# Bucket attention and eight experts on one core: weight pieces that follow ScalarE without a wait, a later closing, sums and opening in other places

## The chip, the core and the metric

The kernel runs on one core of one Trainium2 chip. The core has TensorE (PE, matrix products into PSUM), VectorE (DVE), ScalarE (ACT) and GpSimd (POOL), each with an instruction stream of its own, and SyncE (SP), which here only issues transfers. Semaphores order the streams. The metric is the device time of one execution in microseconds (us), median of the runs shown. "Clock" is the share of full speed that PE's throttle granted.

## The reference

An attention whose mask lets a query see only the keys with the same six sign bits, and behind it a mixture of eight experts of fixed capacity, with a greedy assignment over all scores:

```
q_bits = einsum(q, proj) > 0          # (4, 8, 768, 64) x (64, 6); k_bits alike
mask   = bucket(q_bits) == bucket(k_bits)
scores = where(mask, q @ k.T / 8, -1e9);  attn = softmax(scores);  x = attn @ v   # x: 3072 x 512

logits = x @ w_gate                   # 3072 x 8
for idx in argsort(-logits.flatten()):        # greedy, capacity 384 each
    tok, e = divmod(idx, 8)
    if assigned[tok] >= 0 or counts[e] >= cap: continue
    assigned[tok] = e; counts[e] += 1
for e in range(8):
    out[assigned == e] = relu(x[assigned == e] @ w1[e]) @ w2[e]     # 512 -> 1024 -> 512
```

All is float32. The kernel gets the precision from pairs of 16-bit numbers: a number is split into a high part (a cast, mostly on ACT) and a residue (`lo`, `vl`, `ql`, `kl`, `wl`: number minus high part), and a product is a sum of three 16-bit products.

## The kernel before

**Attention** handles 32 heads in 8 groups of four. A head is six steps (192 in all), each with two half-steps; a half-step is the unit in which the tables count. In a step PE computes one block of masked scores for the row maximum (L239, reduced by DVE in L241) and, some steps later, the transposed scores (`ST`, L257 and L258), whose exponentials ACT takes (L259); the residue `lo` is taken by POOL or DVE (L262), as the tables `PAT`, `E0`, `E1` say by head and step. Four steps later the products with the values follow (L272 to L274). `m_rows` (L243 to L248) writes a head's maxima through PE and ACT into the mask rows of `qa`, which `ST` reads. The three buffers called `pst` in PSUM are shared by `ST`, `m_rows`, the transposed outputs (`xtr`, L299 to L301), the sums and the first routing.

The loads, casts, subtractions and moves of the next group are put between the steps by tables: `P1`, `P2`, `P3` for groups 1 to 3, `P4` for the rest. `sumv` (L194 to L205) sums the values and their residues on PE, and `sumw` (L206 to L213) makes the weights of the mask rows from it: a product, ACT's copy `shi`, and one DVE step. Entry 18 of a table is the half-step of `sumv`, `SW` says how many later `sumw` comes, and `SU` places both for group 0. Before the first step stands the opening, whose order the string `OPS` writes out: `i` constants, `t` `b` casts and sign bits of head 0, `w` warm-up products of PE (no part of the result; `DW` counts a first lot and their width), `r` `l` casts and residues, `s` a score block, `B` `D` bits of head 1 and their transfers, `c` `u` `m` `d` `f` `v` `x` parts of group 0's preparation, `C` copies.

**The first routing** runs inside the last heads: `best` (L485) finds each token's best expert from the logits and makes the key that orders the tokens, in chunks as the batches are done; `compare` (L507) compares a digit of the key with thresholds.

**The experts** are eight blocks of 68 slots: 32 slots of layer 1, 36 of layer 2, three or two PE products in each. While block p-1 runs, the routing of phase p picks the 384 tokens of the next expert, in 14 steps (`phase`, L558) that the tables `EP` and `ES` put at slots: the first is the choice's first count, step 11 is the closing of the search (L636 to L662: the threshold, who is taken, which expert's weights come next), step 12 the places (L665), step 13 the collection (L677), behind which `end` issues the gather of the tokens and begins the next phase's choice. Phases of the table that are not in `EP` use `ES`.

A quarter of a weight matrix is cast by ACT (L757), scaled in place by a second pass of ACT (L766, at the end of `wsplit`), and then split by two pieces `wl`. Pieces wait in a list. `hand` (L771) gives the next n of them to POOL when a routing step has been issued; the counts per step are the tables `HP` (by phase) and `HS`. Ahead of them it puts a `tick` (L774), a copy of one element of the last routing result (`s.gate`), so that POOL does not start before DVE has that result. `fill` and `own` give pieces to DVE, and what is left goes to POOL at a due slot. POOL's queue also holds the scatters of the results (L839), the weight loads (L748) and the gathers (L740).

Of the kernel before, what the change touches and what calls it, by code (L numbers as in the profile page):

```python
# [20 lines left out]
 E0=[3, 5],  # L21
# [5 lines left out]
 DW=[5, 0, 0, 0, 384],  # L27
 P1=[13, 13, 14, 15, 17, 21, 23, 21, 16, 27, 21, 26, 23, 24, 33, 32, 3, 4, 46, -6, 3, 13],
 P2=[41, 44, 48, 49, 51, 51, 57, 55, 45, 49, 55, 57, 52, 60, 59, 60, 2, 3, 72, 32, 36, 47],
# [5 lines left out]
 SW=4,  # L35
# [4 lines left out]
 SU=13,  # L40
 OPS='b0 i3 i2 t0 b1 w5 r0 r2 w4 s0 w4 C1 r1 t1 c1 s1 B0 c0 D0 w2 w1 s4 w5 s2 s3 r3 v2 w5 v0 l0 l1 C0 m0 s5 w3 s6 r5 w2 l3 e0 e1 d0 u0 u1 s7 v1 l2 w0 m1 e2 | s8 | x0 | w0 | x1 s9 | r4 s10 | | | s11 m2 v3 f0 | x3 | | x2 | m3 | | | | | |')
# [4 lines left out]
def attention(tc, nc, ctx, qT, kT, vv, proj, wg, x_dram, L, jp, identf, B, late=None, after=None):  # L46
# [74 lines left out]

    TMP={}
# [8 lines left out]
    def bits(G,pairs):  # L131
# [12 lines left out]
        if G==0: V.tensor_scalar(bt[r],bt[r],8192.0,None,op0=ALU.mult)  # L144
# [172 lines left out]
    def copies(a):  # L317
# [4 lines left out]
        e=lambda k: ST(0,k,0),C=lambda n: copies((QA,KA)[n]),w=lambda n: warm(n,DW[4]))  # L322
# [6 lines left out]
    add(AP['WS'],wsplit); add(AP['SU'],sumv,0); add(AP['SU']+3,sumw,0)  # L329
# [38 lines left out]
    for t in range(6*NH+LAG+6):  # L368
        h,s=divmod(t,6)
        first=(t-LAG)%6==5  # L370
        if first: av(t)
        if t<6*NH and t not in early: ST(h,s,0)
        for x in S_at.get(t,[]): S_pass(*x)
        run(2*t)
        if h<NH: ST(h,s,1)
        if t>=1 and (t-1)//6<NH:
            hh,ss=divmod(t-1,6)
            lo(hh,ss,V if ss in (E0 if hh<1 else E1 if hh<2 else PAT[hh%2]) or t==6*NH else G_)
        run(2*t+1)
        if not first: av(t)  # L380
# [10 lines left out]
ES=[-16,-13,-11,-8,-2,1,5,8,12,15,19,22,28,36]  # L391
EP={1:E1,
# [3 lines left out]
WL=[4,46]  # L396
W1=[[],[57,66,70,74],[53,65,69,73],[50,57,62,67],[46,52,58,63],[44,52,58,63]]
HP={2:[0,0,0,3,1,2,2,2,2,0,0,0,0,0],3:[0,0,0,3,1,2,2,2,2,2,0,0,0,0],4:[0,0,0,3,0,3,0,3,1,2,0,0,0,0]}
HS=[0,0,0,3,0,3,0,2,2,2,0,0,0,0]
# [9 lines left out]
class Moe:  # L409
# [6 lines left out]
    def consts(s):  # L416
# [36 lines left out]
        s.identb=cp.tile([128,128],BF,name="identb")  # L453

        s.gp=cp.tile([128,2,2,NC],BF,name="gp")
        for i,v in enumerate((1.0,-1.0)):
            todo.append(lambda i=i,v=v: A.activation(s.gp[:,i,0,:],iof[:,0:NC],AF.Copy,scale=128.0*v))
            todo.append(lambda i=i,v=v: A.activation(s.gp[:,i,1,:],pcol.to_broadcast([128,NC]),AF.Copy,scale=v))
        s.th=iota([128,4,NC],[[128,4],[0,NC]],0,4097,name="th")
# [10 lines left out]
        todo.append(lambda: G_.tensor_scalar(s.identb,s.jp,0.0,None,op0=ALU.is_equal))  # L470
# [14 lines left out]
    def best(s,P,c0,c1,first=False):  # L485

        V=s.nc.vector; n=c1-c0; r=slice(c0,c1); L3=s.Lm[:,r]
        m,eq,mx,mxu,OH,key,D,E=(P[x] for x in ("m","eq","mx","mxu","OH","key","D","E"))
        def bc(ap): return ap[:,r,None].to_broadcast([128,n,8])
# [5 lines left out]
            lambda: V.tensor_tensor(eq[:,r],eq[:,r],wt,op=ALU.mult),  # L495
# [3 lines left out]
        if not first: todo.append(lambda: V.tensor_tensor(mxu[:,r],mx[:,r],s.un[:,r],op=ALU.mult))  # L499
        return todo+[  # L500
            lambda: V.tensor_tensor(E[:,0,r],D[:,0,r],s.sc[:,0,r],op=ALU.mult),
            lambda: V.tensor_tensor(OH[:,r],bc(mxu),wt,op=ALU.is_equal)]
# [4 lines left out]
    def compare(s,cmp,l,d,c0=0,c1=None,eng=None):  # L507
        J=NT[l]; tb=s.TB[l]
        o,i,b=s.paired(d,c0,s.NC if c1 is None else c1,J,cmp,tb)
        (eng or s.nc.vector).tensor_tensor(o,i,b,op=ALU.is_ge)  # L510

    def paired(s,d,c0,c1,J,out,tb):

        r=slice(c0//2,c1//2); sh=[128,c1//2-c0//2,J,2]
        return out[:,r],d[:,c0:c1].rearrange("p (s q) -> p s q",q=2)[:,:,None].to_broadcast(sh),tb[:,None].to_broadcast(sh)
# [20 lines left out]
    def early(s,b,ps,wps,nb=4):  # L536
# [9 lines left out]
        todo=s.best(s.Z,c0,c0+n,True)  # L546
        for a in range(c0,c0+n,6): todo.append(lambda a=a: s.compare(s.Z["cmp"][0],0,s.Z["E"][:,0],a,a+6))
# [310 lines left out]
    def run(s):  # L858
# [5 lines left out]
        def step(p,n):  # L864
            next(ch[p],None); s.hand(n)
# [82 lines left out]
```

## Time and profile before

| | us |
|---|---|
| median of 3 runs | 735.23 (734.71 to 735.5) |
| the profiled execution | 734.54 |
| its span | 732.8 |
| PE busy in the span | 673.7 (92%) |
| DVE, ACT, POOL busy | 519.3, 470.1, 525.4 |

The mean granted clock is 0.97. Attention with its opening takes until about 393 us, then comes a turn of some 30 us, and layer 1 of the eight blocks starts between 424 and 693 us. A timeline row has the start, the duration, the engine, the line, the operation with its output and inputs, and at the end, in brackets, how long the engine stood idle before it and what ended that. Rows that run without a hole are joined, with their number as x2 and the like.

### The profile page before, as it was taken

Reading aid. Unit: us, or ns where it says so; the run is one execution under the profiler, and the core shown is the slowest. Engines: PE = TensorE matmul, PEld = TensorE weight load, DVE = VectorE, ACT = ScalarE, POOL = GpSimd, SP = SyncE. Lnnn points to the kernel's source line nnn. Section 1 sums busy time; section 2 is a strip of 40 time slices with the busy share of each in tenths; the row PEclk is TensorE's granted clock in tenths of the full one; section 3 lists DMA queues with packets and bytes.
Section 4 is the critical chain, followed back from the end, with each engine's and each line's share of the span. In section 5 each row is a group of like instructions: output and inputs, shape, how many; then the busy total and the mean of one; then the engine's idle time right before and its main releaser. Section 6 shows DMA issues by size and latency. Waiting matters only on the chain. (4 is left out here: it accounts for less than half of the span.)

```text
span 732.8 us, 19247 instructions
## 1 busy us (share of the span) xinstructions
PE 673.7 (92%) x7865; PEld 433.4 (59%) x7865; DVE 519.3 (71%) x1124; ACT 470.1 (64%) x886; POOL 525.4 (72%) x486
## 2 busy tenths in 40 slices
PE   8899989999999999998997599989898989899995
PEld 2566656767767677676675464545454555545552
DVE  5868876878877878788965688697878787843120
ACT  7678776778978788776662172927373645556650
POOL 8589959998988979886772446575756473867761
PEclk9999999999999999999997599999999999999998
DMA  7638572726636255430000344435352526172601
GB/s 194 173 93 229 141 190 50 204 69 134 180 93 165 80 151 158 89 81 23 24 24 23 110 165 147 156 138 179 127 175 98 205 88 229 55 277 58 258 29 43
DMA packets 39952, 93.58 MB, mean 128 GB/s; under 512 B 4548, under 2 KB 30520, under 8 KB 37816
## 3 DMA queue, kind: packets, MB, share of 16 engines
q1 hardware_dynamic: 33048, 46.21, 24.2%
q0 software_dynamic: 6816, 46.15, 18.1%
q8 instruction: 61, 1.00, 0.6%
q14 instruction: 27, 0.22, 0.1%
HBM read 59.53 MB, written 12.58 MB: 98 GB/s over the span
## 5 line engine op out<-in xcount | busy, mean ns | idle before, releaser
L262 POOL TENSOR_TENSOR lo<-pt 128x768 f16<-128x768 f32 x143 | 229.7, 1621 | 40.6 <-ACT pt L259 33.0
L259 ACT ACTIVATE pt<-pst 128x384 f32<-128x384 f32 x384 | 181.1, 491 | 72.9 <-PE pst L258 63.3
L241 DVE TENSOR_REDUCE m<-pss 128x1 f16<-128x770 f32 x192 | 182.0, 957 | 51.8 <-PE pss L239 50.6
L257 PE MATMUL pst<-qa,ka 128*128 128x384 f16 x384 | 126.1, 329 | 7.3 <-ACT qa L248 4.0
L258 PE MATMUL pst<-qb,kb 128*128 128x384 f16 x384 | 125.8, 328 | 0.0
L274 PE MATMUL psv<-vh,lo 128*128 128x65 f16 x1152 | 121.7, 194 | 3.2 <-POOL lo L262 3.2
L273 PE MATMUL psv<-vl,pt 128*128 128x64 f16 x1152 | 121.9, 193 | 0.0
L272 PE MATMUL psv<-vh,pt 128*128 128x65 f16 x1152 | 121.9, 195 | 0.0
L272 PEld LDWEIGHTS <-pt 128*128 128x128 bf16 x1152 | 107.3, 98 | 11.2 <-issue 3.5
L273 PEld LDWEIGHTS <-pt 128*128 128x128 bf16 x1152 | 106.3, 99 | 8.0 <-issue 0.2
L274 PEld LDWEIGHTS <-lo 128*128 128x128 f16 x1152 | 106.3, 98 | 3.5 <-POOL lo L262 3.5
L239 PE MATMUL pss<-ka,qa 128*128 128x385 f16 x384 | 95.0, 330 | 0.4 <-DVE m L241 0.3
L757 ACT ACTIVATE wh<-wf 128x1024 f16<-128x1024 f32 x64 | 67.0, 1051 | 36.6 <-DMA wf<-in_w_dram,zwidx 34.3
L775 POOL TENSOR_TENSOR wl<-wf,wh 128x512 f16<-128x512 f32 x76 | 85.9, 1147 | 0.0
L818 PEld LDWEIGHTS <-wh 128*128 128x128 f16 x512 | 47.9, 98 | 33.4 <-issue 3.4
L830 PEld LDWEIGHTS <-hh 128*128 128x128 f16 x384 | 36.2, 98 | 40.7 <-issue 3.2
L833 ACT ACTIVATE o<-po 128x512 f32<-128x512 f32 x24 | 14.3, 595 | 70.7 <-PE po L830 60.4
L766 ACT ACTIVATE wf<-wf 128x1024 f32<-128x1024 f32 x55 | 58.0, 1055 | 1.0
L262 DVE TENSOR_TENSOR lo<-pt 128x768 f16<-128x768 f32 x49 | 56.8, 1159 | 1.5 <-ACT pt L259 1.0
L821 DVE SCALAR_TENSOR_TENSOR hl<-px,hh 128x384 f16<-128x384 f32 x64 | 34.6, 551 | 30.6 <-ACT hh L820 29.9
L820 ACT ACTIVATE hh<-px 128x384 f16<-128x384 f32 x64 | 31.0, 484 | 37.6 <-PE px L818 34.0
L818 PE MATMUL px<-xh,wh 128*128 128x384 f16 x256 | 53.6, 326 | 1.1 <-DVE xl L794 0.8
(265 smaller groups left out, 1358.5 us busy)
## 6 DMA issues: line engine op xcount, KB each, us to landing
vp<-in_vv_dram SPq DMA_DIRECT2D x8, 768.0 KB
x_dram<-X SPq DMA_DIRECT2D x16, 384.0 KB
qp<-in_qT_dram SPq DMA_DIRECT2D x7, 768.0 KB
kp<-in_kT_dram SPq DMA_DIRECT2D x7, 768.0 KB
qa<-qh SPq DMA_DIRECT2D x14, 192.0 KB
ka<-kh SPq DMA_DIRECT2D x14, 192.0 KB
qb<-qh SPq DMA_DIRECT2D x14, 192.0 KB
kb<-kh SPq DMA_DIRECT2D x14, 192.0 KB
```

The source lines that it names most:

```text
L239: T.matmul(ps[:,hf,0:HK],QA[u][:,j,qc*128:qc*128+128],KA[u][:,j,hf*HK:hf*HK+HK],start=True,stop=True)
L241: V.tensor_reduce(M6[h][:,qc:qc+1],ps[:,:,0:HK],axis=AX.XY,op=ALU.max,negate=True)
L257: T.matmul(ps[:,0:384],KA[u][:,j,kr],QA[u][:,j,r],start=True,stop=False)
L258: T.matmul(ps[:,0:384],KB[u][:,j,kr],QB[u][:,j,r],start=False,stop=True)
L259: A.activation(PT[h,kc][0][:,r],ps[:,0:384],AF.Exp,scale=0.125)
L262: eng.tensor_tensor(l,p,p.bitcast(BF)[:,1::2],op=ALU.subtract)
L272: T.matmul(av[:,c,:],ph[:,r],VH[u][:,j,kc,:],start=(kc==0 and c==0),stop=False,skip_group_check=True)
L273: T.matmul(av[:,c,0:64],ph[:,r],VL[u][:,j,kc,:],start=False,stop=False,skip_group_check=True)
L274: T.matmul(av[:,c,:],l[:,r],VH[u][:,j,kc,:],start=False,stop=False,skip_group_check=True)
L757: s.nc.scalar.mul(h[:,r],f[:,r],WSC)
L775: for _ in range(n): s.nc.gpsimd.tensor_tensor(*s.pend.pop(0)[1],op=ALU.subtract)
L818: T.matmul(p[:,0:384],a[:,o:o+128],b[:,d],start=n==0,stop=n==11)
```

## The change

- Opening: 8 instead of 5 of the first warm-up products, and the others in other places (31 small ones become 27). The scaling of group 0's sign bits by 8192 goes from DVE (L144) to ACT. A tick ahead of POOL's first residue reads an element of the key's sign bits.
- `XL`: heads 4, 7, 8 and 10 have their own list of steps whose `lo` DVE takes: four more than before.
- Sums: `SU` 13 to 15, `sumv` of groups 1 and 2 four and two half-steps later, `sumw` nine half-steps after `sumv` instead of four (group 0: two instead of three).
- First routing (`early`, the chunk of 18 columns): one product goes from DVE to POOL; the equality step and three comparisons read their first operand from PSUM, where a product with a unit matrix (`lift`) puts it.
- Experts: `hand` has no tick except in phase 1 and at the two hands at `dec` in phases 2 and 3. The counts in `HP` and `HS` come earlier. The places stand at slot 29 instead of 28 (`ES`) and 32 instead of 31 (`EP[4]`), the collections at 38, 46 and 41 instead of 36, 44 and 39.

```
- SW=4,
+ SW=9,
+ XL={4:[0,3,5],7:[1,4],8:[0,3,5],10:[0,3,5]},
...
- SU=13,
- OPS='b0 i3 i2 t0 b1 w5 r0 r2 w4 s0 w4 C1 ... B0 c0 D0 ... v2 w5 v0 l0 l1 C0 ...
+ SU=15,
+ OPS='b0 i3 i2 t0 w2 b1 w3 r0 r2 s0 w4 C1 ... B0 c0 a0 D0 ... v2 w5 v0 g0 l0 l1 C0 ...
...
-        if G==0: V.tensor_scalar(bt[r],bt[r],8192.0,None,op0=ALU.mult)
...
+        g=lambda n: G_.tensor_copy(tick,KA[0][64:65,0,0:1]))
...
-    add(AP['WS'],wsplit); add(AP['SU'],sumv,0); add(AP['SU']+3,sumw,0)
+    add(AP['WS'],wsplit); add(AP['SU'],sumv,0); add(AP['SU']+2,sumw,0)
...
-ES=[-16,-13,-11,-8,-2,1,5,8,12,15,19,22,28,36]
+ES=[-16,-13,-11,-8,-2,1,5,8,12,15,19,22,29,38]
...
- 3:[-8,-5,-2,1,5,8,12,15,19,22,26,29,36,44],
- 4:[-12,-9,-6,-3,1,4,8,11,15,18,22,25,31,39]}
+ 3:[-8,-5,-2,1,5,8,12,15,19,22,26,29,36,46],
+ 4:[-12,-9,-6,-3,1,4,8,11,15,18,22,25,32,41]}
...
-HS=[0,0,0,3,0,3,0,2,2,2,0,0,0,0]
+HS=[0,0,2,2,2,0,2,0,2,2,0,0,0,0]
...
-            lambda: V.tensor_tensor(eq[:,r],eq[:,r],wt,op=ALU.mult),
+            lambda: W.tensor_tensor(eq[:,r],eq[:,r],wt,op=ALU.mult),
...
+    def lift(s,ps,a):
+        g=ps()[:,0:a.shape[1]]
+        s.nc.tensor.matmul(g,s.identb,a,start=True,stop=True)
+        return g
...
-            else: todo.append(lambda a=a: s.compare(s.Z["cmp"][0],0,s.Z["E"][:,0],a,a+6))
+            if b==nb-2: todo.append(lambda a=a: s.compare(s.Z["cmp"][0],0,s.lift(ps,s.Z["E"][:,0,a:a+6]),a,a+6,a))
...
-    def hand(s,n):
+    def hand(s,n,wait=True):
...
-        if n: s.nc.gpsimd.tensor_copy(s.z([1,1],F32,"tick"),s.gate)
+        if n and wait: s.nc.gpsimd.tensor_copy(s.z([1,1],F32,"tick"),s.gate)
...
-            next(ch[p],None); s.hand(n)
+            next(ch[p],None); s.hand(n,p==1)
```

POOL's queue in block 4, from the gather of the tokens to the next weight load (`wl` a weight piece, the DMAs `xg` gather, `wf` weight load, `out_dram` scatter), first before:

```order
272 L740 DMA xg<-x_dram,zidx 128x512 x3
273 L748 DMA wf_10907<-in_w_dram,zwidx 128x4096
274 L774 CAST ztick<-zcmp_391 1x1
275 L775 TENSOR_TENSOR wl_10910<-wf_10770,wh_10909 128x512 x3
276 L839 DMA out_dram<-o,zidx 3072x512
277 L774 CAST ztick<-zcmp_392 1x1
278 L775 TENSOR_TENSOR wl_10910<-wf_10770,wh_10909 128x512 x3
279 L839 DMA out_dram<-o,zidx 3072x512
280 L774 CAST ztick<-zcmp_391 1x1
281 L775 TENSOR_TENSOR wl_11104<-wf_10907,wh_11103 128x512 x2
282 L774 CAST ztick<-zcmp_391 1x1
283 L775 TENSOR_TENSOR wl_11104<-wf_10907,wh_11103 128x512 x2
```

and after:

```order
246 L750 DMA xg<-x_dram,zidx 128x512 x3
247 L758 DMA wf_10880<-in_w_dram,zwidx 128x4096
248 L785 TENSOR_TENSOR wl_10883<-wf_10743,wh_10882 128x512 x4
249 L849 DMA out_dram<-o,zidx 3072x512
250 L785 TENSOR_TENSOR wl_10883<-wf_10743,wh_10882 128x512 x2
251 L849 DMA out_dram<-o,zidx 3072x512
252 L785 TENSOR_TENSOR wl_11073<-wf_10880,wh_11072 128x512 x6
253 L849 DMA out_dram<-o,zidx 3072x512
254 L758 DMA wf_11238<-in_w_dram,zwidx 128x4096
```

The ticks are gone, the first scatter stands behind four pieces instead of three, and the six pieces of the second matrix stand in one row.

ACT's queue around the third group's sums (`sq` ends `sumv`, `shi` is the copy of `sumw`, L248 and L249 the mask rows, `XT` a transposed output, `pt` exponentials), before:

```order
163 L205 COPY sq<-pst 128x256
164 L259 ACTIVATE pt<-pst 128x384
165 L128 CAST kh<-kp 128x384
166 L259 ACTIVATE pt<-pst 128x384 x3
167 L212 CAST shi<-pst 32x256
168 L248 ACTIVATE qa_173<-pst,mbi,msc 32x384
169 L259 ACTIVATE pt<-pst 128x384 x2
170 L300 CAST XT<-pst 128x384
171 L259 ACTIVATE pt<-pst 128x384 x2
172 L300 CAST XT<-pst 128x384
173 L259 ACTIVATE pt<-pst 128x384
```

and after:

```order
163 L206 COPY sq<-pst 128x256
164 L260 ACTIVATE pt<-pst 128x384
165 L130 CAST kh<-kp 128x384
166 L260 ACTIVATE pt<-pst 128x384 x3
167 L249 ACTIVATE qa_176<-pst,mbi,msc 32x384
168 L260 ACTIVATE pt<-pst 128x384 x2
169 L301 CAST XT<-pst 128x384
170 L260 ACTIVATE pt<-pst 128x384 x2
171 L301 CAST XT<-pst 128x384
172 L260 ACTIVATE pt<-pst 128x384
173 L213 CAST shi<-pst 32x256
```

The copy no longer stands ahead of the mask rows; it follows the second transposed output.

## Rows read from the trace of the kernel before

**Rows 1.** the page, section 1: busy us (share of span) x instructions
```profile
PE 673.7 (92%) x7865; PEld 433.4 (59%) x7865; DVE 519.3 (71%) x1124; ACT 470.1 (64%) x886; POOL 525.4 (72%) x486
```

**Rows 2.** PE's waits, whole span: us in total, times, longest
```profile
PE pst L203 <- POOL vl L192: 4.1, 3, 2.1
PE pst L257 <- ACT qa L248: 4.0, 7, 0.6
PE pst L257 <- DVE XT L301: 2.5, 2, 1.3
```

**Rows 3.** PE's waits from 424 to 733 us
```profile
PE psa L677 <- DVE zRr L701: 5.3, 4, 2.1
PE psa L665 <- DVE zwidx L732: 4.8, 4, 1.8
PE psa L665 <- DVE zSTb L649: 1.3, 1, 1.3
PE po L830 <- POOL wl L775: 0.9, 2, 0.7
```

**Rows 4.** timeline, DVE, closing of phase 5: start, us, engine, line, op, out<-in
```profile
595.12 3.63 DVE L644 SCALAR_TENSOR_TENSOR zwg<-zd,znn,zmxu 128x24 f32<-128x24 bf16 x1
```

**Rows 5.** line L644, all phases: count: ns min/median/max, first and last start
```profile
L644 DVE SCALAR_TENSOR_TENSOR zwg<-zd,znn,zmxu x7: 233/2332/3631, 408.7 to 634.0; 128x24 f32<-128x24 bf16 x7
```

**Rows 6.** timeline, POOL, the same stretch
```profile
594.10 2.26 POOL L775 TENSOR_TENSOR wl<-wf,wh 128x512 f16<-128x512 f32 x2
596.45 2.25 POOL L775 TENSOR_TENSOR wl<-wf,wh 128x512 f16<-128x512 f32 x2
```

**Rows 7.** line L510 on DVE
```profile
L510 DVE TENSOR_TENSOR zcmp<-psa,tb x30: 945/957/959, 430.1 to 630.2; 128x768 bf16<-128x768 f32 x30
```

**Rows 8.** timeline, PE, places of phase 5
```profile
599.47 0.20 PE L665 MATMUL psa<-zSTb,ntri 128*128 128x48 bf16 x1 [1.75 <-DVE zwidx L732]
```

**Rows 9.** windows: stretch, us, busy (x) by engine, PEclk, DMA, GB/s
```profile
600.20:603.60 3.40, 3.40 (x12) 1.47 (x10) 3.37 (x9) 0.15 (x1) 0.96 (x1) 0.50 0.75 198
```

**Rows 10.** timeline, ACT, last pass but one of phase 5
```profile
590.99 1.06 ACT L766 ACTIVATE wf<-wf 128x1024 f32<-128x1024 f32 x1
```

**Rows 11.** timeline, PE, collection of phase 3 to first product of phase 4
```profile
529.45 0.79 PE L677 MATMUL psa<-zRr,ohp 128*128 128x12 bf16 x24 [2.14 <-DVE zRr L701]
...
535.34 0.76 PE L521 MATMUL psa<-zOH,zcmp 128*128 128x8 bf16 x24
```

**Rows 12.** timeline, POOL, group 1's last value residue
```profile
68.64 1.60 POOL L192 TENSOR_TENSOR vl<-vp,vh 128x384 f16<-128x384 f32 x1
```

**Rows 13.** timeline, PE, group 1's sum
```profile
70.28 0.27 PE L203 MATMUL pst<-vl,on 128*32 128x256 f16 x1 [1.70 <-POOL vl L192]
```

**Rows 14.** timeline, ACT, the first cast of the next loads
```profile
36.96 0.92 ACT L128 CAST qh<-qp 128x384 f16<-128x384 f32 x2 [0.20 <-DMA qb<-qh]
```

**Rows 15.** timeline, ACT, group 3: the copy of sumw
```profile
153.34 0.36 ACT L212 CAST shi<-pst 32x256 f16<-32x256 f32 x1 [0.21 <-PE pst L209]
```

**Rows 16.** timeline, PE, behind that copy
```profile
154.44 0.32 PE L257 MATMUL pst<-qa,ka 128*128 128x384 f16 x1 [0.65 <-ACT qa L248]
```

**Rows 17.** timeline, DVE, the first routing
```profile
333.47 1.61 DVE L495 TENSOR_TENSOR zeq<-zeq,wt 128x144 f32<-128x144 f32 x1
```

**Rows 18.** timeline, DVE, opening
```profile
8.49 1.27 DVE L224 TENSOR_SCALAR qa<-qa 6x768 f16<-6x768 f16 x1
```

**Rows 19.** timeline, POOL, opening
```profile
7.92 1.63 POOL L230 TENSOR_TENSOR qb<-XT,qb 64x768 f16<-64x768 f32 x1
```

**Rows 20.** timeline, ACT, end of the opening
```profile
21.76 0.66 ACT L248 ACTIVATE qa<-pst,mbi,msc 32x384 f16<-32x384 f32 x1 [5.97 <-issue]
```

**Rows 21.** the page, section 5: line, xcount | busy, mean ns | idle before
```profile
L262 DVE TENSOR_TENSOR lo<-pt 128x768 f16<-128x768 f32 x49 | 56.8, 1159 | 1.5 <-ACT pt L259 1.0
```

**Rows 22.** timeline, POOL, ahead of 108 us
```profile
107.68 1.64 POOL L130 TENSOR_TENSOR ql<-qp,qh 128x768 f16<-128x768 f32 x1 [7.92 <-DMA qb<-ql]
```

**Rows 23.** line L757 on ACT: idle before it until, us, times
```profile
  DMA wf<-in_w_dram,zwidx: 34.3, 7
```

More of the change, by code (lines that the diff above doesn't have):

```diff
@@ L119, in attention @@
         WF.append(cp.tile([128,4,65],F16,name=f"wf{u}")); G_.memset(WF[u],0.0)
+    tick=cp.tile([1,1],F32,name="tick")
     TMP={}
@@ L321, in attention @@
         m=lambda n: m_rows(n//2,n%2),d=lambda n: dm(0,[1]),f=lambda n: dm2(0,[1]),v=lambda j: cv(0,j),x=lambda j: sv(0,j,G_),
-        e=lambda k: ST(0,k,0),C=lambda n: copies((QA,KA)[n]),w=lambda n: warm(n,DW[4]))
+        e=lambda k: ST(0,k,0),C=lambda n: copies((QA,KA)[n]),w=lambda n: warm(n,DW[4]),a=lambda n: bscale(0),
+        g=lambda n: G_.tensor_copy(tick,KA[0][64:65,0,0:1]))
     n=-1; early=[]
@@ L483, in ps, with best @@
     def ps(s): return s.psA.tile([128,512],F32,name="psa")
-    def best(s,P,c0,c1,first=False):
-        V=s.nc.vector; n=c1-c0; r=slice(c0,c1); L3=s.Lm[:,r]
+    def best(s,P,c0,c1,first=False,ps=None):
+        V=s.nc.vector; W=s.nc.gpsimd if ps else V; n=c1-c0; r=slice(c0,c1); L3=s.Lm[:,r]
         m,eq,mx,mxu,OH,key,D,E=(P[x] for x in ("m","eq","mx","mxu","OH","key","D","E"))
@@ L501, in best, with compare, paired @@
             lambda: V.tensor_tensor(E[:,0,r],D[:,0,r],s.sc[:,0,r],op=ALU.mult),
[L502 removed]
+            lambda: V.tensor_tensor(OH[:,r],s.lift(ps,mxu[:,r])[:,:,None].to_broadcast([128,n,8]) if ps else bc(mxu),wt,op=ALU.is_equal)]
+    def lift(s,ps,a):
+        g=ps()[:,0:a.shape[1]]
+        s.nc.tensor.matmul(g,s.identb,a,start=True,stop=True)
+        return g
     def digit(s,P,l,r):
         s.nc.vector.tensor_scalar(P["D"][:,l,r],P["key"][:,r],SH[l],(1<<WID[l])-1,op0=ALU.logical_shift_right,op1=ALU.bitwise_and)
[L507 removed]
+    def compare(s,cmp,l,d,c0=0,c1=None,off=0):
         J=NT[l]; tb=s.TB[l]
[L509 to L512 removed]
+        o,i,b=s.paired(d,c0,s.NC if c1 is None else c1,J,cmp,tb,off)
+        s.nc.vector.tensor_tensor(o,i,b,op=ALU.is_ge)
+    def paired(s,d,c0,c1,J,out,tb,off=0):
         r=slice(c0//2,c1//2); sh=[128,c1//2-c0//2,J,2]
[L515 removed]
+        return out[:,r],d[:,c0-off:c1-off].rearrange("p (s q) -> p s q",q=2)[:,:,None].to_broadcast(sh),tb[:,None].to_broadcast(sh)
     def count(s,pc,P,cmp,l,c0,c1):
@@ L545, in early @@
             s.Z["cmp"]=[s.z([128,NC//2,32 if i else NT[0],2],BF,f"cmp{i}",bufs=1) for i in range(3)]
-        todo=s.best(s.Z,c0,c0+n,True)
-        for a in range(c0,c0+n,6): todo.append(lambda a=a: s.compare(s.Z["cmp"][0],0,s.Z["E"][:,0],a,a+6))
+        todo=s.best(s.Z,c0,c0+n,True,ps if b==nb-2 else None)
+        for a in range(c0,c0+n,6):
+            if b==nb-2: todo.append(lambda a=a: s.compare(s.Z["cmp"][0],0,s.lift(ps,s.Z["E"][:,0,a:a+6]),a,a+6,a))
+            else: todo.append(lambda a=a: s.compare(s.Z["cmp"][0],0,s.Z["E"][:,0],a,a+6))
         if b==nb-1:
```

16 lines of the change are left out of this document (8 added, 8 removed).

## The prediction

> **What bounds the kernel now.** I read the share of busy time first: TensorE (PE) works 92% of the span, and no other engine is over 72% [rows 1]. So PE is the bound, and the change adds only four small products to its work and takes four warm-up products away; a gain can only come from PE's idle time (about 59 us with the head and the tail) or from its clock. The waits of PE, grouped by the line that waited and by its releaser, say where that idle time is. In attention three groups touch lines of the change: the sums of the value residues wait for POOL's residue, the masked scores wait for ScalarE's (ACT) mask rows, and they wait twice for a transposed output that DVE delivers [rows 2]. In the expert stage the largest groups are the two steps that close a routing phase: the places L665 and the collection L677 wait for DVE [rows 3]. Then I read single stretches for the reason of each.
>
> **The expert stage: why the closing steps wait.** In phase 5, DVE's L644, a step on 24 elements per partition, is in the record for 3.63 us [rows 4]. The same step takes from 0.23 to 3.63 us over seven phases, median 2.33 [rows 5]. Over exactly that time POOL runs two pairs of weight pieces, 594.10 to 596.36 and 596.45 to 598.70, one piece 1.13 us [rows 6]; L644 starts at 595.12 and ends 0.05 us after the last piece. The scores that are read from PSUM never stretch: 30 of them lie between 945 and 959 ns [rows 7]. So a DVE step whose operands are all in SBUF stands still while POOL streams pieces, and PE's places at 599.47 come 1.75 us late [rows 8]. PE's clock then falls: in 600.2 to 603.6 the granted clock is 0.50, the 1.2 GHz level, though PE is busy throughout [rows 9].
>
> The Trainium skill ("SBUF — State Buffer", section "Who interferes with whom") says that a DVE instruction with two SBUF inputs contends with a GpSimd instruction that reads SBUF, that one with at most one does not, and that whoever issues first holds the pair for its whole instruction. The PSUM half agrees with the trace. By its one-instruction lock a closing could lose at most one piece, 1.13 us; the trace has 3.63, some three pieces, so the measurement decides. By the rule a closing that still meets pieces after the change would lose about 1.1 and not 3.6.
>
> The change takes the waits of the hands (the "tick" that reads the routing's last result) away from phase 2 on, except the two after the places of phases 2 and 3. It counts no piece in the step just before a closing, and keeps the number of pieces on POOL and on DVE. A piece then starts when ACT's scaling pass is done. In phase 5 the last pass but one starts at 590.99 and takes 1.06 [rows 10]; two pieces behind it end near 592.05 + 2.26 = 594.3, before L644's 595.1, with 0.8 us to spare. So I take the waits of the closings as gone: 5.3 + 4.8 + 1.3 = 11.4 us (the four collections, four places and the place that shows its wait under L649) [rows 3]. The 0.9 us in which PE waits for a POOL piece goes too, since pieces come earlier. The 3.4 us at half clock would be 1.7 at full clock; without the 1.75 us hole before it I count 1.5 of this as won.
>
> What it adds. First, collections stand two slots later (36 to 38, 44 to 46, 39 to 41), while the next phase starts where it did. Between a collection and the next phase's first product PE had 12 slots, 529.45 to 535.34 or 5.9 us, 0.49 a slot, and DVE's chain of the next choice filled just that time [rows 11]. With 10 slots (4.9 us) phase 4's first product is 1.0 late, with 11 (5.4) phase 5's is 0.5 late, and with 14 the later ones are not: +1.5. The gathers behind these collections start later by the same two slots, which I price at zero, 1.0 at most in one phase. Second, the ticks had kept pieces behind the end of a comparison; now they can fall on any DVE step whose operands are in SBUF, and on DVE's own weight pieces. One such meeting costs between nothing and 3.6 us; I take half a piece, 0.5, for five phases and two own pieces: +3.5. The expert stage: -11.4 - 0.9 - 1.5 + 1.5 + 3.5 = -8.8, with ends at -13.8 (no meeting, no late start) and about -3 (half of the closings still wait).
>
> **Attention: the sums.** PE waits 4.1 us in three places for POOL's value residue, 2.1 the longest [rows 2]. In the second group the last residue ends at 70.24 [rows 12] and PE, standing since 68.58, goes on at 70.28 after 1.70 [rows 13]; the sum is moved four half-steps later, and a half-step is about one microsecond (384 of them in some 380 us), so PE arrives past 72 and waits no more: -1.7. In the first group the sum moves two half-steps later, past the casts of the next loads, and the first of these casts already waits 0.20 us, to 36.96, for a DMA that frees its buffer [rows 14]. ACT stands there with the mask rows queued behind, so I expect PE to wait for that instead of the residue: 0, with ends at -2.1 and +2. The last part of the sums (`sumw`) is moved from 4 to 9 half-steps behind the first. Before, its copy on ACT at 153.34 stands right ahead of the mask rows [rows 15] and PE loses 0.65 us behind them [rows 16]; of the seven such waits (4.0 us in all) [rows 2] five have a `sumw` in their step, four of 0.65 and one of 0.53: -3.1. In groups 1 to 3 the new place is beside a transposed output and I take 0.6 back: -2.5.
>
> **Attention: the first routing.** The choice of the first phase starts inside attention, and its mask product takes 1.61 us on DVE while POOL streams residues [rows 17]; behind it PE waits for DVE's output, twice, 2.5 us in all [rows 2]. The product goes to POOL, and the comparisons read a copy in PSUM, where a comparison takes 0.96 [rows 7]. I take 2.0 of the 2.5; the four products that lift the operands to PSUM are under 0.2 us each and use buffers that the masked scores share (0 to +0.8, counted 0).
>
> **Attention: opening and four residues.** DVE's scaling of the sign bits took 1.27 us beside POOL's first residue [rows 18], which started at 7.92 [rows 19]. Now POOL waits until both have been scaled, which I put about 4 us later; PE first computes masked maxima that read no residue, and the first products that read a residue come after them, so I take this as hidden. The scaling that moves to ACT stands there ahead of a cast and two copies, and ACT was idle for 5.97 us ahead of its mask rows at 21.76 [rows 20]: hidden, but the bits' DMAs go out some 0.5 later, since ACT takes longer for it than DVE. Fewer warm-up products (31 to 27 of the small ones) can leave the clock lower for longer. +0.5, between -1 and +3. Four score residues go from POOL to DVE, 1.16 each there [rows 21]; DVE is idle 29% of the span: 0. The largest POOL wait of attention stays, since POOL stands 7.92 us for a DMA there [rows 22] whose place is not changed.
>
> **Sum.** Attention +0.5 - 1.7 + 0 - 2.5 - 2.0 = -5.7, expert stage -8.8, together -14.5. The profiled execution took 734.54 us (span 732.8), 0.7 under the median of 735.23: 734.54 - 14.5 = 720.0 against its own time, 720.7 as a median. I forecast 721 us.
>
> **Rivals.**
> 1. The stalls only move: ticks were a brake, and without them POOL runs six pieces in a row; they hit the first comparison, DVE's own pieces or the choice of the next phase, and a stream held a step for three pieces once. For it: [rows 4, 6], and less room behind the collections. Against: the steps in between read PSUM. Half of the expert gain goes: -4.4 - 5.7, about 725.
> 2. Attention gives nothing: in the first group the wait passes to the DMA, in the others to the next buffer of the ring. For it: [rows 14, 22]. Against: the five waits behind `sumw` have their reason in their own step. 734.5 - 8.8 + 0.7, about 726.5.
> 3. Slower: POOL's queue. Without the tick the first piece of a quarter stands at the head of POOL's queue until ACT's pass, and ACT waits for weights, 34.3 us in seven places [rows 23]. Behind it stand the scatter and the next weight load; if the load goes out a pass and two pieces later (1.06 + 1.06 + 2.26 = 4.4 us) and the weights are then missing by that much in each of five blocks, 22 us are lost against 14.5 won: 742. It decides from 2.9 us a block. Against: a tick waited just as well in that queue, and PE never waited for a scaled weight of ACT in this stage.
> 4. It does not do what it says: pieces still cover the closings since ACT's passes end later than I worked out (0.8 us to spare in phase 5), and attention's waits only change names. About 735.
>
> Chances: my forecast 0.60 (its own range 715 to 726), rival 1 0.18, rival 2 0.10, rival 3 0.07, rival 4 0.05. The range 713 to 730 takes in the first three and the ends of the unknown costs. A run of this kernel tells a difference of about 0.2%, 1.5 us. Faster by more than that: 0.60 + 0.18 + 0.10 and a part of rival 4, 0.89; within it 0.04; slower 0.07.
>
> **What would show it.** Right: L644, L646, L647 and the collection's first step at 0.2 us from phase 2 on, but for the hands after the places in phases 2 and 3; PE's waits under L665 and L677 (moved lines) below 4 us in all; no half clock near 600; no 0.65 us waits behind ACT's mask rows; no wait for the value residue at 70. Wrong: a new wait of PE for ACT's mask rows or a DMA at 37, long DVE steps at the start of a phase, PE waiting for `wl` or ACT for weights longer than before, or the half clock staying on longer in the opening.

## The result, and the profile after

| | before | changed |
|---|---|---|
| median, us | 735.37 (4 runs, 734.71 to 738.93) | 717.2 (4 runs, 714.78 to 720.31) |
| ratio, 95% interval | | 0.9753 [0.9732, 0.9774] |
| profiled execution, span | 734.54, 732.8 | 718.04, 716.3 |

The changed kernel is faster by 18.2 us in the medians and by 16.5 in the profiled executions. Between these two, PE's busy time falls by 4.6 us, 3.1 of it in the opening up to row 12 of the table below, and its idle time by 11.9. Busy time on the page of the changed kernel, against [rows 1]:

```profile
PE 669.1 (93%) x7868; PEld 432.4 (60%) x7868; DVE 516.9 (72%) x1126; ACT 471.4 (66%) x887; POOL 517.1 (72%) x456
```

Where the time went is read from PE's own milestones, the starts of the same products in both traces. "Row n" is PE's n-th block of masked scores (L239, now L240; six to a head, from 0), "scores n" the n-th step of the transposed scores (L257, now L258), "block k" the first product of layer 1 of block k.

| PE's milestone | before | changed | difference | the stretch's own |
|---|---|---|---|---|
| row 12 (opening) | 28.58 | 25.41 | -3.2 | -3.2 |
| scores 12 (group 0's sums) | 48.65 | 48.36 | -0.3 | +2.9 |
| row 48 (group 1) | 103.02 | 101.87 | -1.2 | -0.9 |
| row 60 (the hole at 110.8) | 130.39 | 126.40 | -4.0 | -2.8 |
| scores 156 (groups 3 to 6) | 325.20 | 321.38 | -3.8 | +0.2 |
| scores 180 (first routing) | 370.87 | 365.05 | -5.8 | -2.0 |
| block 0 (the turn) | 424.00 | 420.49 | -3.5 | +2.3 |
| block 3 | 543.79 | 536.56 | -7.2 | -3.7 |
| block 6 | 659.36 | 643.28 | -16.1 | -8.9 |
| last product's end | 723.80 | 707.73 | -16.1 | 0.0 |

From block 0 to the end the expert stage takes 287.2 instead of 299.8 us: -12.6.

PE's waits there, from 409 to the end, answer to [rows 3]:

```profile
PE px L828 <- ACT xh L815: 2.4, 1, 2.4
PE psa L687 <- DVE zRr L711: 1.8, 2, 0.9
PE psa L529 <- DVE zcmp L518: 0.7, 1, 0.7
```

The closing step of [rows 5] now (L654), and a timeline of the closing of phase 5 against [rows 4, 6, 8]:

```profile
L654 DVE SCALAR_TENSOR_TENSOR zwg<-zd,znn,zmxu x7: 232/234/679, 403.9 to 621.3; 128x24 f32<-128x24 bf16 x7
```

```profile
579.00 6.72 POOL L785 TENSOR_TENSOR wl<-wf,wh 128x512 f16<-128x512 f32 x6
586.31 0.23 DVE L654 SCALAR_TENSOR_TENSOR zwg<-zd,znn,zmxu 128x24 f32<-128x24 bf16 x1
...
593.33 0.79 PE L687 MATMUL psa<-zRr,ohp 128*128 128x12 bf16 x24
```

POOL has done its six pieces at 585.72, 0.6 us ahead of the closing step, which takes 0.23; the places start without a wait and so does the collection, and the granted clock is 1.00 from 590 to 620. The groups L665 and zSTb of [rows 3] are gone from the list, and of the 5.3 us under L677 1.8 are left, in phases 2 and 3, where a hand with its tick still follows the places. Two things are new in the expert stage. Layer 2 waits once for VectorE's residue `hl`. And three of DVE's own weight pieces (at 531, 566 and 601) run beside one of POOL's; there it is POOL's piece that takes longer, 1.39 to 1.69 us instead of 1.15, while DVE's takes 0.69 as ever (PE, then DVE and POOL at the third of them):

```profile
558.43 0.39 PE L840 MATMUL po<-wh,hl 128*128 128x512 f16 x1 [1.07 <-DVE hl L831]
...
600.93 0.69 DVE L794 SCALAR_TENSOR_TENSOR wl<-wf,wh 128x512 f16<-128x512 f32 x1
600.97 2.78 POOL L785 TENSOR_TENSOR wl<-wf,wh 128x512 f16<-128x512 f32 x2 [0.98 <-ACT wf L776]
```

The opening in the changed kernel (PE, the first lot of warm-up products, then the sign-bit products L223 and the first score block), and its sign-bit products before:

```profile
1.20 3.45 PE L76 MATMUL psv<-wrm 128*128 128x512 f16 x8 [1.20 <-DVE c L88]
5.18 1.45 PE L223 MATMUL pst<-XT,prt 64*6 64x384 f32 x4 [0.53 <-DMA prt<-in_proj_dram]
...
7.00 1.45 PE L223 MATMUL pst<-XT,prt 64*6 64x384 f32 x4
...
9.59 0.49 PE L240 MATMUL pss<-ka,qa 128*128 128x385 f16 x2 [0.55 <-DVE ka L225]
```

```profile
5.14 5.28 PE L222 MATMUL pst<-XT,prt 64*6 64x384 f32 x8 [1.64 <-DMA prt<-in_proj_dram]
```

Four of these products take 1.45 us instead of 2.64 (half of the row's 5.28), so PE is at the upper of its two clock levels when they start, and the first score block stands at 9.59 instead of 13.16. Below this is the early clock; where four of these products take 2.6 to 2.7 us, the clock is late.

Group 0's sums in the changed kernel, ACT's cast and PE behind it, and the window with the granted clock behind that (0.55):

```profile
34.53 0.93 ACT L130 CAST qh<-qp 128x384 f16<-128x384 f32 x2 [3.62 <-DMA kb<-kl]
36.20 0.37 PE L204 MATMUL pst<-vh,on 128*32 128x256 f16 x1 [3.30 <-ACT qa L249]
```

```profile
34.40:42.00 7.60, 5.80 (x63) 4.13 (x63) 1.98 (x3) 5.93 (x13) 4.08 (x3) 0.55 0.33 108
```

ACT stands 3.62 us at the first cast of the next loads, up to the transfers that free its buffer, and PE stands 3.30 behind it. The 2.1 us wait for the residue [rows 2] has become this longer one.

Two places further on: the second group's sum no longer waits [rows 13], but the score product behind it waits for a transfer; and the transfer on which POOL stood to 107.68 [rows 22] lands at 104.47, so that the hole at 110.8 shrinks from 3.16 to 0.67 us (in order: PE, POOL, PE).

```profile
71.01 0.32 PE L259 MATMUL pst<-qb,kb 128*128 128x384 f16 x1 [1.86 <-DMA qb<-ql]
...
104.47 1.65 POOL L132 TENSOR_TENSOR ql<-qp,qh 128x768 f16<-128x768 f32 x1 [5.07 <-DMA qb<-ql]
107.60 0.20 PE L275 MATMUL psv<-vh,lo 128*128 128x65 f16 x1 [0.67 <-POOL lo L263]
```

In the turn into the expert stage, ACT's second cast of the tokens comes late, and PE with it. The reason is not in the rows: the profile puts ACT's 2.95 us down to a PE product that this cast doesn't read. Behind PE's wait the granted clock is 0.50, from 420.8 to 424.2:

```profile
418.32 0.60 ACT L815 ACTIVATE xh<-px 128x512 f16<-128x512 f32 x1 [2.95 <-PE psa L814]
420.49 0.84 PE L828 MATMUL px<-xh,wh 128*128 128x384 f16 x3 [2.36 <-ACT xh L815]
```

### The profile page after: what moved, and what is told of

The parts are those of the page before. It is cut to its first block, busy times and chain, and to the rows that moved or that the text cites. A ratio compares the mean times of both kernels' runs of the same rounds, so it can differ in the third digit from the quotient of the medians.

```text
span 716.3 us, 19197 instructions
## 1 busy us (share of the span) xinstructions
PE 669.1 (93%) x7868; PEld 432.4 (60%) x7868; DVE 516.9 (72%) x1126; ACT 471.4 (66%) x887; POOL 517.1 (72%) x456
## 3 DMA queue, kind: packets, MB, share of 16 engines
q0 software_dynamic: 6816, 46.15, 18.2%
## 5 line engine op out<-in xcount | busy, mean ns | idle before, releaser
L263 POOL TENSOR_TENSOR lo<-pt 128x768 f16<-128x768 f32 x139 | 224.3, 1626 | 47.4 <-ACT pt L260 43.0
L258 PE MATMUL pst<-qa,ka 128*128 128x384 f16 x384 | 125.4, 327 | 2.5 <-ACT qa L249 1.3
L240 PE MATMUL pss<-ka,qa 128*128 128x385 f16 x384 | 94.6, 329 | 1.4 <-DVE m L242 0.6
L767 ACT ACTIVATE wh<-wf 128x1024 f16<-128x1024 f32 x64 | 67.0, 1052 | 34.9 <-PE psa L735 20.9
L263 DVE TENSOR_TENSOR lo<-pt 128x768 f16<-128x768 f32 x53 | 73.4, 1385 | 1.6 <-ACT pt L260 1.0
L240 PEld LDWEIGHTS <-qa 128*128 128x128 f16 x384 | 37.2, 97 | 27.8 <-issue 1.5
```

The lines of the kernel that those rows point to most:

```text
L240: T.matmul(ps[:,hf,0:HK],QA[u][:,j,qc*128:qc*128+128],KA[u][:,j,hf*HK:hf*HK+HK],start=True,stop=True)
L258: T.matmul(ps[:,0:384],KA[u][:,j,kr],QA[u][:,j,r],start=True,stop=False)
L263: eng.tensor_tensor(l,p,p.bitcast(BF)[:,1::2],op=ALU.subtract)
L767: s.nc.scalar.mul(h[:,r],f[:,r],WSC)
```

## The experiments

Each is timed beside the kernel before on the same chip. A median of four runs of one kernel moves by some 2 us, and one reason shows in the first pair, so what a single edit does is read from the milestones of the profiled executions, and the medians stand beside. The milestones have a spread of their own. Kernels 5 to 8 have the attention code of the changed kernel; the five take 20.7 to 23.0 us from row 12 to scores 12 and 24.5 to 27.5 from row 48 to row 60, the changed kernel's profile being the longest in the one and the shortest in the other. From row 60 to scores 156 they agree within 0.1 us. The eight kernels with the changed expert part (the changed one, 1 to 4 and 9 to 11) take 286.2 to 287.3 us from block 0 to the end.

**1 and 2. The opening as before; and only its first lot.**

```
open_back:  DW[0] 8 -> 5, OPS as before, bits scaled on DVE, no tick g0
lot5:      - DW=[8, 0, 0, 0, 384],   + DW=[5, 0, 0, 0, 384],
```

> The changed kernel with the whole opening as before (5 first warm-up products, the old order, the sign bits scaled by VectorE, no tick ahead of GpSimd's first residue). Theory A, the clock: the opening won 3.6 us because TensorE's full clock came before the sign-bit products (L223: 1.45 us for four instead of about 2.6). Then the first score block starts near 13.2 us again, not 9.6. Theory B, rival: the time after the opening is set by the transfers of group 0's second pair (the cast at 34.5 waits for them), which are paced by TensorE's steps, so nearly all of the 3.6 us comes back as later end: total +2 to +4 us on the changed kernel (719 to 721). Theory C: the transfers are not paced by TensorE, the hole at 36 us shrinks by what the opening loses, and the total is within 1 us of the changed kernel (717).

> The changed kernel with 5 instead of 8 first warm-up products, all else of the opening as changed. If the three extra products raise the clock early (theory A), the sign-bit products take 2.6 us for four again, the first score block starts 2.5 to 3.5 us later than 9.6, and the granted clock is at half until about 13 us. If the new order of the rest raises it (rival), the first score block stays at 9.6 to 10.5 us and the time does not change.

Measured: 721.27 (718.16 to 723.18) and 721.02 (718.52 to 721.95). The sign-bit products of the one and of the other:

```profile
5.32 5.28 PE L224 MATMUL pst<-XT,prt 64*6 64x384 f32 x8 [1.80 <-DMA prt<-in_proj_dram]
```

```profile
5.19 2.72 PE L223 MATMUL pst<-XT,prt 64*6 64x384 f32 x4 [1.67 <-DMA prt<-in_proj_dram]
```

The first score blocks start at 13.26 and 12.44. So the three extra warm-up products make the early clock; without them PE stands 1.67 us ahead of the products, with them 0.53. The rest of the new order gives 0.8 us at the first score block and nothing at the first transposed scores (23.07 with the old order, 23.88 with the new one and a lot of 5). At row 12 the two kernels are 3.3 and 4.1 us behind the changed one, at the last product 4.9 and 2.6, so what of the opening's gain reaches the end is known to about 2 us; theory B of the first expectation is the nearer one, and its 13.2 for the first score block came too. But the early clock is not certain. Ten of the profiled kernels have a first lot of 8 or more with this order. In eight of them the clock was up at the first sign-bit products or just behind their start, in two it was not, as in the fourth experiment:

```profile
5.18 2.72 PE L223 MATMUL pst<-XT,prt 64*6 64x384 f32 x4 [0.39 <-DMA prt<-in_proj_dram]
```

There the first score block stands at 12.44 and the first transposed scores at 27.08 instead of 19.81, later than before the change (22.98). None of the four with a lot of 5 had the early clock.

**3 and 4. Group 0's sums where they were; and the casts behind the wait moved.**

```
su13:         SU 15 -> 13, sumw 3 behind
casts_later:  P1=[13,13,14,15,17,21,23,21, 16,27,21,26, ... -> [17,17,18,19,19,21,23,21, 18,27,21,26, ...
```

> The changed kernel with group 0's sums where they stood before (13 and 3 behind). Theory A: the casts' wait for the transfer that ends at 34.5 us stops ScalarE, and TensorE waits behind it wherever the sums stand; then the hole of 3.3 us at 36 is replaced by a wait for the value residue at about 32 of 1 to 2 us and TensorE's step at 36 is at most 1 us earlier; total 716 to 718. Theory B: moving the sums behind the casts made the hole; then it is 2 us or less, the half clock from 34 to 42 gets shorter, and the total falls to 714 to 715.5.

> The changed kernel with the first four casts of group 1 moved four to five half-steps later (13, 13, 14, 15 to 17, 17, 18, 19; the next cast and the first residue from 17 and 16 to 19 and 18). Theory A: the wait of the first cast for the transfers that free its buffer (to 34.5 us) is what stops ScalarE and TensorE behind it; then the 3.3 us hole at 36 goes, the half clock from 34 to 42 with it, and group 0 ends 3 to 6 us earlier, of which 2 to 5 us stay in the total (712 to 715). Theory B: the wait only moves on to the moves of group 1, whose transfers come later by the same time (the hole at 71 grows); total within 1 us of 717.

Measured: 715.28 (714.52 to 717.39), ratio to before 0.9732 [0.97, 0.9765], and 716.59 (713.38 to 717.94). PE in the first of them:

```profile
32.12 0.27 PE L204 MATMUL pst<-vl,on 128*32 128x256 f16 x1 [1.27 <-POOL vl L193]
...
35.74 0.32 PE L258 MATMUL pst<-qa,ka 128*128 128x384 f16 x1 [0.76 <-ACT qa L249]
```

The hole is 1.27 and 0.76 us instead of 3.30, no half clock follows, and from row 12 to scores 12 this kernel takes 19.31 us where the changed one takes 22.95 and kernels 5 to 8 take 20.7 to 22.0: theory B of the third expectation holds, moving the sums was a loss of 1.4 to 3.6 us there. Part of it is given back later (a hole of 2.31 us at 104.38 instead of 0.67, with a granted clock of 0.50 from 104.7 to 108.1); 2.2 us are left at the end. With the casts moved instead there is no wait of PE between 38.4 and 46 us and the same stretch takes 17.81. Its profiled execution had the late clock, so it started 7.3 us behind and ended 0.1 ahead of the changed kernel: theory A for the stretch. That the opening kept its median (716.59) above theory A's 712 to 715 is shown for one of its four executions alone.

The hole itself comes every time: it is 2.8 to 3.9 us in all nine kernels that have sums and casts as changed, also behind the old opening (3.91 in experiment 1), and gone in both that move the casts (4 and 12). The half clock behind it does not come every time. In experiment 8, with the same code up to there, PE's wait is 3.26 us, and the window that reads 0.55 in the changed kernel reads

```profile
34.40:42.00 7.60, 5.29 (x90) 3.86 (x90) 2.99 (x7) 6.36 (x15) 4.11 (x3) 1.00 0.32 108
```

**5, 6 and 7. Ticks back, counts back, both back.**

```
ticks_back:   - next(ch[p],None); s.hand(n,p==1)   + next(ch[p],None); s.hand(n)
counts_back:  HP and HS as before
ticks_counts_back:  both
```

> The changed kernel with the tick ahead of every hand again; the counts per step and the slots stay as changed. Theory A, the ticks held GpSimd's pieces until the closings: the pieces start after a comparison again, VectorE's closing steps (L654, L656, L657) stretch to 2 to 3.6 us in several phases, and of the 12.6 us that the expert stage won 5 to 9 come back: 722 to 726. Theory B, the counts alone keep the pieces away from the closings: the closing steps stay at 0.2 us and the total within 1.5 us of the changed kernel (716 to 718.5).

> The changed kernel with the counts per step of before, still without ticks (from phase 2 on), slots as changed. Theory A (the ticks were what held the pieces; without them a piece starts when ScalarE's pass is done, whatever step hands it out): closings stay at 0.2 us but for at most one phase, total within 1.5 us of the changed kernel. Theory B (pieces handed out late stand behind scatters and start late all the same): closings stretch in three or more phases, total 721 to 725.

> The changed kernel with both the ticks and the counts of before, slots as changed. Read from layer 1 of block 0 to the end (287.2 us in the changed kernel, 299.8 before; 290.1 with the ticks alone back, 286.4 with the counts alone back). Theory A, either edit alone suffices for most of the gain and both together are what made the stalls: 296 to 300 us, closing steps at 2 to 3.6 us in four or more phases. Theory B, the later places and collections hid a part by themselves: 291 to 294 us.

Measured: 724.05 (721.62 to 728.62), 716.23 (714.86 to 722.03) and 730.29 (729.41 to 733.72, 7 runs). From block 0 to the end: 290.1, 286.4 and 299.3 us, against 287.2 in the changed kernel and 299.8 before. The closing step in the three:

```profile
L654 DVE SCALAR_TENSOR_TENSOR zwg<-zd,znn,zmxu x7: 233/823/2767, 406.9 to 626.4; 128x24 f32<-128x24 bf16 x7
```

```profile
L654 DVE SCALAR_TENSOR_TENSOR zwg<-zd,znn,zmxu x7: 232/234/444, 402.9 to 619.3; 128x24 f32<-128x24 bf16 x7
```

```profile
L654 DVE SCALAR_TENSOR_TENSOR zwg<-zd,znn,zmxu x7: 232/2330/3635, 405.7 to 632.3; 128x24 f32<-128x24 bf16 x7
```

With both back the closing of phase 5 is that of [rows 4, 6] again:

```profile
593.38 2.26 POOL L785 TENSOR_TENSOR wl<-wf,wh 128x512 f16<-128x512 f32 x2
594.40 3.63 DVE L654 SCALAR_TENSOR_TENSOR zwg<-zd,znn,zmxu 128x24 f32<-128x24 bf16 x1
595.73 2.26 POOL L785 TENSOR_TENSOR wl<-wf,wh 128x512 f16<-128x512 f32 x2
```

So the whole gain of the expert stage hangs on ticks and counts, and either edit alone brings most of it: the counts alone 9.2 us of 12.0 (299.3 - 290.1), the ticks' removal alone all of it. Of the fifth expectation neither theory holds: the ticks cost 2.9 us, since with the counts as changed four closings still stand, but for 0.8 to 2.8 us and not, as with both back, five for 2.3 to 3.6. The profiled execution of `ticks_back`, 724.02, was also 2.8 us behind at block 0, with the late clock. In the sixth theory A holds, in the seventh theory A.

**8. Places and collections at their old slots.**

```
slots_back:  ES places 29 -> 28, collections 38 -> 36, 46 -> 44, 41 -> 39, EP[4] places 32 -> 31
```

> The changed kernel with places and collections at the slots of before (28 and 36, phase 3 at 36 and 44, phase 4 at 31 and 39). Theory A: with the stalls gone the earlier slots suffice, the late starts of phases 4 and 5 (waits of 0.74 and 0.33 us under L529) go, and nothing comes: -1 to 0 us. Theory B: the closing's chain on VectorE needs the two slots; TensorE waits 0.3 to 0.8 us at the places and at the collection of each of phases 2 to 6: +2 to +5 us (719 to 722).

Measured: 720.09 (714.45 to 722.54). Its profiled execution is the shortest of the four, and there block 0 to the end takes 285.9, 1.4 less than in the changed kernel and 0.3 less than in the shortest of the eight with the changed slots. The late start of phase 4 in the changed kernel, 0.74 us, is gone in it; the collections wait 2.7 us instead of 1.8 (a timeline row of the changed kernel, then PE's waits of this one):

```profile
528.17 0.58 PE L529 MATMUL psa<-zOH,zcmp 128*128 128x8 bf16 x17 [0.74 <-DVE zcmp L518]
```

```profile
PE psa L687 <- DVE zRr L711: 2.7, 3, 1.7
```

Both of that expectation's theories have a part, theory A the larger one. Also gone is layer 2's wait of 1.07 us for `hl`: all ten experiments that have the later slots show it (2.63 us in 7), and neither this one nor the kernel before nor 12 does. With the stalls gone the later slots cost more than they give, some 1 us by two profiles (285.9 here, 285.5 in 12). The median with its spread of 8 us settles nothing.

**9. The expert part alone, on the kernel before.**

> The kernel before with the expert part of the change alone (ticks, counts, slots), attention and opening as before. Theory A, the parts add up: the expert stage wins 12.6 us as in the changed kernel, total 722 to 723.5. Theory B, part of the expert stage's gain hangs on where attention leaves the weight loads and the clock: 10 us or less, 725 or more. If the 2.3 us that the turn into the expert stage lost in the changed kernel (TensorE waits 2.36 us for ScalarE's cast of the tokens at 420) is due to the expert part, it shows here too.

Measured: 720.52 (719.4 to 722.71), ratio 0.9803 [0.976, 0.9845]. From block 0 to the end 286.6 us, 13.2 less than before: theory A, the expert gain does not need the rest. Its median is 3.3 us above that of the changed kernel, so some 3 us are what opening and attention have left at the end. In the turn PE waits only 1.80 us for the tokens and not for ACT, so the 2.36 us are not the expert part's.

**10. The four score residues back on POOL.**

```
xl_back:  - AP['XL'].get(hh,PAT[hh%2])   + PAT[hh%2]
```

> The changed kernel without the four score residues moved from GpSimd to VectorE. Theory A, the 3.2 us hole at 110.8 went because GpSimd has fewer residues around heads 7 to 10: it is back with 2 us or more and the half clock behind it, total 719 to 722. Theory B, it went because the transfers that GpSimd waits for (to 104.5 instead of 107.7) land earlier against TensorE's steps, which the opening and group 0 decide: the hole stays within 0.7 us of that of the changed kernel where the opening is as fast, total within 2 us.

Measured: 718.87 (714.78 to 724.15). PE's waits for POOL's residues:

```profile
108.02 0.20 PE L275 MATMUL psv<-vh,lo 128*128 128x65 f16 x1 [1.45 <-POOL lo L263]
...
122.83 0.20 PE L275 MATMUL psv<-vh,lo 128*128 128x65 f16 x1 [1.16 <-POOL lo L263]
```

The first hole is 1.45 instead of 0.67 and a second of 1.16 us comes; the half clock behind them does not. Row 48 to row 60 takes 1.6 us more, 26.1. But kernels 5 to 8, which have the four residues where the change put them, show the first hole with 1.21 to 2.66 us and take 25.1 to 27.5: this difference is within what one execution differs from the next. Only the second hole is in no other kernel. Theory A falls, theory B is the nearer one (the hole is 0.1 outside its 0.7 us), and what the four residues give is not shown beyond that second hole.

**11. `sumw` and the first routing as before.**

```
sw4_lift_back:  SW 9 -> 4; equality and comparisons read SBUF, product on DVE
```

> The changed kernel with the last part of the sums 4 half-steps behind the first again, and with the first routing's product and comparisons as before. By stage: the 0.65 us waits behind the mask rows are back at about 152, 208, 253, 297 and 340 us, and the waits for the transposed output (1.1 and 1.35 us) between 325 and 365. Theory A, each is a direct loss of TensorE: from block row 60 to row 156 of the scores (126.4 to 305.6 in the changed kernel) +1.3 to +2.0 us, from there to row 180 +1.7 to +2.3. Theory B, the waits stand for others that come in their place (VectorE's maxima and transposed outputs): under half of that.

Measured: 717.42 (716.27 to 720.16). The two kinds of wait are back, as in [rows 2]; one of each:

```profile
207.49 0.32 PE L258 MATMUL pst<-qa,ka 128*128 128x384 f16 x1 [0.65 <-ACT qa L249]
...
356.62 0.32 PE L258 MATMUL pst<-qa,ka 128*128 128x384 f16 x1 [1.35 <-DVE XT L302]
```

But from row 60 to row 156 this kernel takes only 0.8 us more than the changed one, in spite of four waits of 0.65 and one of 0.96 us, and from there to scores 180 1.8 more: theory B for `sumw`, theory A for the routing. Even the 0.8 us is not the waits behind the mask rows: the kernel before, with the same four waits, takes 179.2 us from row 60 to row 156, as the changed one does; the 0.96 us wait is in neither. The turn is 2.8 us shorter here (no wait for ACT at 420), which hides both in the total: from scores 156 to block 0 this kernel takes 98.3 us and the changed one 99.1.

**12. A version that takes from them.** The changed kernel with the casts of 4, the slots of 8 and a first lot of 10.

> The changed kernel with three more edits: the first casts of group 1 four to five half-steps later (as in casts_later), places and collections at the slots of before (as in slots_back), and 10 instead of 8 first warm-up products, so that TensorE has no hole before the sign-bit products. Theory A, the gains add: casts -5 in attention, slots -1.4 in the expert stage, and the extra warm-up products make the early full clock the usual case (L223 1.45 us for four): 709 to 712. Theory B, the early clock stays a toss and the transfers of group 1 take back what the casts gave: 713 to 716.

Measured: 712.09 (710.86 to 716.58), ratio to before 0.97 [0.9662, 0.9737], against 0.9753 [0.9732, 0.9774] of the changed kernel. The page and the sign-bit products:

```profile
PE 666.8 (94%) x7870; PEld 430.7 (61%) x7870; DVE 516.1 (73%) x1126; ACT 470.2 (66%) x887; POOL 516.0 (73%) x456
```

```profile
5.58 1.85 PE L223 MATMUL pst<-XT,prt 64*6 64x384 f32 x4
```

PE no longer stands ahead of these products, which start 0.4 us later, and the first score block stands at 10.37, 0.8 later than with a lot of 8. From row 12 to scores 12 it takes 17.7 us, 2.9 to 5.2 less than the five kernels with the changed attention, and block 0 to the end takes 285.5. Theory A for the casts and the slots. Whether ten warm-up products make the early clock safe is open: one of its four runs, at 716.58, lies 5 us above the others' middle, and has no trace.

## Why the prediction was right, and where it was not

The time, 717.2, lies in the range (713 to 730) and in the forecast's own range (715 to 726), 3.8 under the 721 forecast. The bound, the place of the main gain and its mechanism were right: DVE's closing steps stood still under POOL's pieces. Experiments 5 to 7 show it by bringing the stalls back. Its size was -12.6 against -8.8. The gains of 11.4 + 0.9 + 1.5 came for the most part: of the collections' 5.3 us 1.8 stayed, in phases 2 and 3, though the two hands that keep their tick there were named, and of the 0.9 for a POOL piece 0.6. The half clock near 600 is gone, but it is there in the first products of block 0, behind the turn (0.50 from 420.8 to 424.2). The cost term of +3.5 for pieces that meet other DVE steps was the one mis-sized: the first comparisons take 1.75 us at most, as before, and where DVE's own pieces meet POOL's, it is POOL's that wait. So that a DVE step with all operands in SBUF stands still beside POOL's pieces was put too widely; in the expert stage only the closing steps and the collection's first step do. The late starts (+1.5) measured 0.74 + 0.33; that the later collections hold up `hl` and with it layer 2, 1.07 us, was not foreseen.

The spare time in phase 5 was forecast as 0.8 us and is 0.6. What hangs on the Trainium skill's rule ("SBUF — State Buffer", section "Who interferes with whom") came out against it again: a one-instruction lock would have let the step go after 1.13 us at most, but in experiment 7 the step stood 3.63 us, through the rest of one pair of pieces and the whole next pair, with 0.09 us between the pairs.

The attention's sum, -5.7, measured -5.8 to scores 180, but by other terms, so it was right by chance:

- Opening: +0.5 forecast (-1 to +3), -3.2 measured, where the clock comes early. The step that failed read the fewer small warm-up products as a risk for the clock and left the three more of the first lot out of the count; they close most of PE's hole ahead of the sign-bit products, and experiment 2 shows that they are the reason. In two profiles of ten the late clock came all the same.
- Group 0's sums: 0 forecast (-2.1 to +2), +2.9 measured in this pair, 0.6 to 2.9 over the five kernels with this attention code. That ACT's stand at the transfer takes the residue's place was foreseen; its length was not, and the half clock behind it was not counted. The opening's lead (PE came there 3.2 us earlier, the transfer 2.4) does not explain the length: with the old opening the hole is 3.91 us.
- Group 1's sum: the wait of 1.70 went as forecast, but 1.86 us for a transfer came right behind it; the stretch to row 48 won 0.9.
- The hole at 110.8 was said to stay, because POOL's transfer is not moved. It shrank, and no half clock follows: the transfer landed 3.2 us earlier while PE came 0.7 earlier. How much is this profile's luck shows in kernels 5 to 8, where the hole is 1.21 to 2.66 us (and 3.85 in experiment 9, which has the attention of before); what the four residues, priced at 0, gave of it is open (experiment 10).
- `sumw`: -2.5 forecast, 0 to -0.8 measured. The waits went as named, the four of 0.65 us, yet from row 60 to row 156 the kernel before takes no more (179.2 us in both), and experiment 11 takes 0.8 more. Counting each wait as a loss of PE was the error: smaller waits for VectorE's maxima and outputs stood behind them.
- First routing: -2.0 forecast, -2.0 measured up to scores 180, and so by experiment 11. At block 0 nothing of it is seen: from scores 156 to there the kernel before takes 98.8 us and the changed one 99.1.

What was not seen at all is the turn, +2.3. It has no edit of its own; kernels 1, 9 and 11 do not have ACT's late cast (each has another instruction stream there), the others have it with 0.5 to 2.4 us or, in 10, a wait of 0.8 us that the profile gives no releaser. Ten of the eleven kernels with the new first routing have it and none of the three without, but that the new routing causes it is not shown. Its cause is open.

Rival 1 (the stalls only move) falls with the first comparisons and DVE's own pieces at their old durations. Rival 2 was right on group 0's transfer, on group 1, where a transfer took the residue's place, and mostly on `sumw`; it was wrong on the opening and the first routing. Rival 3 (POOL's queue) did not come: PE waits 0.6 us for a piece in the whole stage, and ACT's waits for weights did not grow (10.0 us by name and 20.9 in the turn, against 34.3 in [rows 23]). Of the signs of being wrong one came, PE's wait behind ACT's mask rows at 36. And that a run tells a difference of 1.5 us was too bold: four runs of one kernel spread by 3 to 9 us here.

## What to carry to other kernels

A small step that takes ten or fifteen times its usual time is a stall and not work: look at what the neighbour engine streams in exactly that time, and move the stream (here by starting it when its data is ready) rather than the step. A queue that is held back by a wait "for tidiness" comes out as a block where it hurts most; two edits that each cure it don't add up, so each has to be undone alone and both together. And an earlier start is worth only what the next transfer lets through: price the next wait in line, with the clock that may fall behind it. Before one profile's stretch is set against another's, look how far that stretch differs between kernels that have the same code there.

## What the runs showed of the hardware

- The clock's rise in the opening is not the same in every execution of nearly one program: with 8 or 10 first warm-up products the first four sign-bit products took 1.45 to 1.85 us in eight profiles and 2.72 us in two. In the fourth experiment the lower level lasted to about 23 us, which is 7.3 us at the first transposed scores; in the fifth it is 3.4. This is likely one reason why four runs of one of these kernels spread by 3 to 9 us; only one run of each has a trace.
- The granted clock of the windows misses this: in that fourth experiment it reads 1.00 from 5 to 22 us while the products take nearly twice their time (2.72 us for four instead of 1.45). In an opening, read the duration of a known product instead.
- A wait of PE of 3.3 us can cost more than itself, and need not: from 34.4 to 42 the granted clock was 0.55 around the 3.30 us of the changed kernel, 0.78 around 2.88 us in experiment 6 and 1.00 around 3.26 us in experiment 8, all three with the same attention code.
- Not every DVE step that reads SBUF alone stands still beside POOL. A DVE weight piece that began 0.04 us ahead of POOL's kept its 0.69 us, and POOL's took 1.67. The closing steps waited for the end of the stream, even where one had begun 0.8 us ahead of its first piece, while POOL issued a scatter (kernel before: L647 at 558.63 for 3.10 us, pieces from 559.43 to 561.69).
